# Taps of the last channels through a 128-row operand, dummy matmuls, and the order of two loads in the opening of a convolution and FFN kernel

## The chip, the cores and the metric

The kernel runs on one core of one Trainium2 chip. The metric is the device time of one execution in microseconds (us). The engines are named as in the profile: PE is TensorE's matmuls and PEld its weight loads, DVE is VectorE, ACT is ScalarE, POOL is GpSimd, SP is SyncE; a q behind the name (SPq, ACTq) is the instruction queue of that engine, where its DMAs are issued.

## The reference

Two layers run one after the other, each twice. With S = 2048 positions, D = 576 channels and F = 4608:

```python
x = A_q
x = x + A(layernorm(x), A_k, A_v, shift_k, ssm_k, ssm_D)
x = x + B(layernorm(x), w_gate, w_up, w_down)
x = x + A(layernorm(x), A_k, A_v, shift_k, ssm_k, ssm_D)
x = x + B(layernorm(x), w_gate, w_up, w_down)

# A: a causal convolution of four taps on k, times v; a long causal convolution; a gate
k_shift[s] = sum over t < 4 of k[s - t] * shift_k[:, t]      # per channel
kv = k_shift * v
y  = causal convolution of kv with ssm_k (length S), by FFT  +  kv * ssm_D
A  = q * y
# B: (gelu(x @ w_gate) * (x @ w_up)) @ w_down
```

All inputs are bf16.

## The kernel before, in words

The 2048 positions are worked on in four blocks of 512, and each block's rows as 128 partitions by four rows (`RT = 4`). The long convolution is done block by block by discrete Fourier transforms written as matmuls with tables of sines and cosines (`W` and `Wx`). The FFN's weights are streamed, and its matmuls take up nearly all of TensorE's time. A hand-written planner with cost estimates (the `Pace` object) interleaves the later blocks' convolution with the FFN of earlier blocks. The opening is different: `Conv.begin` (L856) writes its order out by hand, and the scheduling is manual, so each engine runs its instructions in the order of the text. `begin` uses no planned times, so the planner's decisions after it do not depend on what is in it.

What `begin` does, up to the point where the dense work starts:

- **Loads.** ScalarE's queue asks for `sk9` (L887, the taps as nine rows of 64 channels, given twice) and then for `dv9` (L889, D in the same form). SyncE's queue asks for the first block of k (L179, called at L888), for h, the first 512 positions of `ssm_k`, with channels on the partitions: `hn` in 4 x 128 rows (L894) and then the last 64 rows (L895); for v (L188), the tables W (L897), x (L1237), Wx (L899), the rest of W (L900), then four DMA transposes `hx` (L902) and the first FFN weights (L1224 to L1226). The semaphores by which the loads report are taken in turn.
- **Dummies.** `busy` (L912) makes matmuls of ones by ones, 256 columns each, into a tile that nobody reads (L914): ten at the start, two later.
- **Taps.** Four matmuls of the nine-row `sk9` (L920) give the taps of the first 384 channels as columns, from which VectorE makes diagonal matrices `dg` (L926). For the last 192 channels three matmuls (L931) spread a row of taps to all 128 partitions: the stationary operand is one column of the identity, broadcast, and the moving operand is the nine rows of `sk9`. ScalarE copies that to `sx` (L935).
- **k.** When k has landed, two matmuls with a shifted identity (L941) give the neighbours' rows, which ScalarE copies to `kx` (L951); twelve transposes (L949) turn the first 384 channels, which ScalarE copies to `kT` (L954), in two goes.
- **h.** `turn_h` (L978) transposes `hn` in ten pieces (L985), eight of 128 rows and two of the last 64, for two of the four row classes i at a time, and ScalarE copies the result to `hT0` (L988). In the first call `turn_d` (L959) comes between: a small transpose of `dv9` (L962) into a tile that already holds transposed k, ScalarE's copies to `dcol` (L964), and GpSimd's addition of D to the column of `hn` for time 0 (L966). The second call's half with i = 0 reads that column.
- **Convolution of four taps.** For the first 384 channels `shift_taps` (L839) multiplies by the diagonal matrices on TensorE, seven matmuls for each of three groups of 128 channels (L843); the second call of `turn_h` stands between the first and the second group. VectorE does the last 192 channels itself from `kx` and `sx` (L970 to L976), and then multiplies TensorE's results by v (L1010).
- Then come the transforms of h and of kv (L235, L242), their products, the inverse transforms (L429), the gate, the norm and the first FFN matmuls (L1708).

The matmul that the change rewrites in the taps:

```python
nc.tensor.matmul(ps[:, c // 2, c % 2 * HP * KS:(c % 2 + 1) * HP * KS],
                 lhsT=self.ident[0:NH, 2 * nt + c:2 * nt + c + 1].to_broadcast([NH, P]),
                 rhs=sk9[:, 0, :], start=True, stop=True)
```

Here `P` is 128, `NH` = 9, `HP` = 64, `KS` = 4, `nt` = 3 and c runs over the three rows of 64 channels that make up the last 192.

Of the kernel before, what the change touches and what calls it, by code (L numbers as in the profile page):

```python
# [18 lines left out]
BF16 = mybir.dt.bfloat16  # L19
# [3 lines left out]
P = 128  # L23
BS = 512
# [68 lines left out]
class Conv:  # L93
# [762 lines left out]
    def begin(self, head, tables):  # L856

        tc, nc, D, KS = self.tc, self.nc, self.D, self.KS
        nd = D // P
        width = lambda db: min(P, D - db * P)  # L860
        with ExitStack() as es:
            tmp = es.enter_context(tc.tile_pool(name="s_tmp", bufs=1))
            HP = P // 2
            NH = D // HP
            sk9 = tmp.tile([NH, 2, HP * KS], BF16, name="sk9")
            dv9 = tmp.tile([NH, 2, HP], BF16, name="dv9")
            sk9t = tmp.tile([NH, KS, HP], BF16, name="sk9t")
            hx = tmp.tile([P, RT, D], BF16, name="hx")
            dcol = tmp.tile([P, nd + 1], F32, name="dcol")
            nt = nd - 1  # L870
            DW = D - nt * P
# [5 lines left out]
            hn = tmp.tile([P, nd + 1, BS], BF16, name="hn")  # L877
# [6 lines left out]
            ones = lambda n: nc.const_aps.tensor(1.0, [P, n], BF16)  # L884

            twice = lambda src: src.unsqueeze(1).to_broadcast([NH, 2, src.shape[1]])
            nc.scalar.dma_start(out=sk9[:], in_=twice(self.sk.rearrange("(b p) j -> b (p j)", p=HP)))  # L887
            self.load_k(0, nc.sync)  # L888
            nc.scalar.dma_start(out=dv9[:], in_=twice(self.sD.rearrange("(b p) -> b p", p=HP)))  # L889
            nc.vector.memset(kT[:, :, :, 0:2], 0.0)  # L890
            nc.vector.memset(below[:, 0:1], 0.0)
            nc.vector.tensor_copy(out=below[:, 1:P], in_=self.ident[:, 0:P - 1])
            nc.scalar.activation(out=warm[:], in_=ones(1), func=ACT.Sqrt)
            nc.sync.dma_start(out=hn[:, 0:nd, :], in_=self.hk[0:nd * P, 0:BS].rearrange("(b p) t -> p b t", p=P))  # L894
            nc.sync.dma_start(out=hn[0:D - nd * P, nd, :], in_=self.hk[nd * P:D, 0:BS])  # L895
            self.load_v(0, nc.sync)
            nc.sync.dma_start(out=self.W[:, 0:12, :], in_=tables[:, 0:12, :])  # L897
            head.more(0)
# [13 lines left out]
            def busy(ps, n):  # L912
                for _ in range(n):
                    nc.tensor.matmul(ps[:, 0, 0:256], lhsT=ones(P), rhs=ones(256), start=True, stop=True)  # L914
            idle = small()
# [13 lines left out]
            ps = new()  # L929
            for c in range(DW // HP):  # L930
                nc.tensor.matmul(ps[:, c // 2, c % 2 * HP * KS:(c % 2 + 1) * HP * KS],  # L931
                                 lhsT=self.ident[0:NH, 2 * nt + c:2 * nt + c + 1].to_broadcast([NH, P]),
                                 rhs=sk9[:, 0, :], start=True, stop=True)
            for e, (lo, hi) in enumerate(((0, P), (P, DW))):
                nc.scalar.copy(out=sx[:, :, lo:hi], in_=ps[:, e, 0:(hi - lo) * KS].rearrange("p (d j) -> p j d", j=KS))  # L935
            busy(idle, 2)
            k, v = self.kt_[0], self.vt_[0]
            rest = slice(nt * P, D)
            px = new()
# [4 lines left out]
            for n, dbs in enumerate(DBS):  # L944
                pt = new_t() if n else small_t()
# [6 lines left out]
            for dbs, pt in zip(DBS, pts):  # L952
                ne = len(dbs)
                nc.scalar.copy(out=kT[:, dbs[0]:dbs[-1] + 1, :, 2:P + 2],  # L954
                               in_=pt[:, 0:ne, 0:RT * P].rearrange("p e (u q) -> p e u q", u=RT))
# [22 lines left out]
            def turn_h(pt, g, first=None):  # L978

                hv = hn[:].rearrange("p b (q i) -> p b i q", i=RT)  # L980
                for dbs in (range(nd), (nd,)):
                    for i in (2 * g + 1, 2 * g):
                        for db in dbs:
                            w = width(db)
                            nc.tensor.transpose(pt[:, i % 2, db * P:db * P + w], hv[0:w, db, i, :], self.ident[0:w, 0:w])  # L985
                if first:
                    first()
                nc.scalar.copy(out=hT0[:, 2 * g:2 * g + 2, :], in_=pt[:, :, 0:D])  # L988

            turn_h(new_t(), 1, lambda: turn_d(pts[1]))  # L990
            out = []
            for n, dbs in enumerate(DBS):
                o = (new() if n else small())[:].rearrange("p e (i c) -> p e i c", i=RT)
                for e, db in enumerate(dbs):
                    self.shift_taps(k, kT, dg, P, db, o[:, e])
                    if db == 0:
                        turn_h(new_t(), 0)
                out.append(o)
# [38 lines left out]
            def take(dst, ps, s, copy=None):  # L1037
                (copy or nc.scalar.copy)(out=self.halves(dst[:, s, :]), in_=ps[:, :, 0:HW])  # L1038

            def first(which, src, kt, s, ps):  # L1040
                if s == 0 and which is kc:
                    for k in (kt, kt + 2):
                        kc[k] = self.kcp.tile([P, 2, D], BF16, tag="kc", name="kc")
                T[src is v, kt, s] = ps
                for e in range(2):
                    self.fwd_sum(ps, src, kt, s, e)
                take(which[kt], ps, s)
# [904 lines left out]
```

## Time and profile before

| what | value |
|---|---|
| median of 3 runs | 905.81 us (905.8 to 905.88) |
| the profiled execution's own time | 905.94 us |
| its span, first to last instruction | 904.1 us |
| TensorE matmuls busy | 899.0 us, 99% of the span, 8127 instructions |
| VectorE / ScalarE / GpSimd busy | 556.9 / 329.6 / 157.9 us |
| first dense matmuls of the transform of kv | 12.64 us after the start of the span |
| first FFN matmul | 32.58 us |

The profile is one execution taken by the hardware profiler. Its views: the page (shares and groups), the chain of work that ended last, the timeline of each engine, the waits (who waited for whom), the DMA issues with the time to landing, and windows (busy time of each engine in a stretch). Times in the views are microseconds from the first instruction. In a timeline row stand the start, the length of the merged group, the engine, the line, the operation, the tiles (out<-in), the shapes and the count, and in brackets the idle time before it with what ended it. The ends of matmuls are modelled; a group's length includes the last one's tail, so the distance from one group's start to the next says more about its speed.

### The profile page before, as it was taken

How to read it: one execution, taken by the hardware profiler on the slowest of the kernel's cores; microseconds unless marked ns; L12 is line 12 of the kernel's file. 1: busy time of each engine (PE TensorE's matmuls, PEld its weight loads, DVE VectorE, ACT ScalarE, POOL GpSimd, SP SyncE). 2: the span in 40 equal slices, each digit the busy share in tenths (PEclk: the TensorE clock that was granted, in tenths of full speed). 3: DMA queues.
4: the chain of work that ended last, by engine and by line, in shares of the span. 5: the costliest groups of instructions: out<-in, count | busy, mean ns of one | idle time of the engine just before them, and what ended most of it. 6: DMA issues, size and time to landing. Idle time of an engine off the chain costs nothing.

```text
span 904.1 us, 19109 instructions
## 1 busy us (share of the span) xinstructions
PE 899.0 (99%) x8127; PEld 524.5 (58%) x8127; DVE 556.9 (62%) x957; ACT 329.6 (36%) x616; POOL 157.9 (17%) x336
## 2 busy tenths in 40 slices
PE   9999999999999999999999999999999999999998
PEld 7875646556466465564654655644444477754466
DVE  8989977678988884887898855443333322123311
ACT  7775455423322255443115133553323313022310
POOL 4423315020223031510104002310000012000000
PEclk9999999999999999999999999999999999999999
DMA  9999998567639219766915501965454431249700
GB/s 274 293 308 327 185 253 143 166 197 168 190 90 263 85 27 181 217 128 137 269 54 135 129 3 40 192 134 106 132 105 132 100 72 27 58 124 227 185 7 20
DMA packets 132075, 133.03 MB, mean 147 GB/s; under 512 B 46139, under 2 KB 123670, under 8 KB 131990
## 3 DMA queue, kind: packets, MB, share of 16 engines
q1 hardware_dynamic: 121728, 94.79, 46.7%
q0 software_dynamic: 10208, 37.02, 12.8%
q8 instruction: 63, 1.03, 0.5%
q14 instruction: 22, 0.18, 0.1%
q10 hardware_dynamic: 54, 0.01, 0.0%
HBM read 108.49 MB, written 12.39 MB: 134 GB/s over the span
## 4 chain that ended last, share of the span: by engine, by line
PE 97%; ACT 1%; DMA 0%; DVE 0%; issue 0%; DVEq 0%
PE gu L1872 60%; PE dn L1747 31%; PE gu L1708 3%; PE cps L296 1%; PE ps L235 1%; PE ps L296 0%; PE ps L429 0%; PE cps L429 0%; DMA k<-in_A_k_dram 0%; PE cps L843 0%; PE cps L235 0%; DVE v L1010 0%; PE xps L1507 0%; ACT junk L1268 0%; ACT kc L1038 0%; ACT x_c L1567 0%
## 5 line engine op out<-in xcount | busy, mean ns | idle before, releaser
L1872 PE MATMUL gu<-xnT,wgu 64*128 64x512 bf16 x4968 | 539.4, 376 | 0.0
L1872 PEld LDWEIGHTS <-wgu 64*128 64x128 bf16 x4968 | 240.2, 94 | 294.4 <-issue 4.3
L1881 ACT ACTIVATE ga<-gu 128x512 f32<-128x512 f32 x258 | 154.0, 597 | 403.9 <-PE gu L1872 395.6
L1882 DVE TENSOR_TENSOR hT<-ga,gu 128x512 bf16<-128x512 f32 x258 | 177.1, 686 | 198.8 <-ACT ga L1881 197.5
L1747 PE MATMUL dn<-wd,hT 128*128 128x288 bf16 x2304 | 290.9, 286 | 0.0
L1747 PEld LDWEIGHTS <-hT 128*128 128x128 bf16 x2304 | 224.0, 98 | 63.0 <-issue 6.4
L1260 POOL TENSOR_SCALAR nm<-s 128x1 f32<-128x1 f32 x56 | 20.4, 364 | 261.6 <-DVE x_c L1778 201.7
L1268 ACT ACTIVATE junk<-x_c,nm 128x576 bf16<-128x576 f32 x48 | 37.0, 770 | 44.9 <-POOL nm L1260 43.9
L1769 DVE TENSOR_TENSOR ob<-x_c,dn 128x576 bf16<-128x576 f32 x15 | 11.3, 754 | 67.6 <-PE dn L1747 67.6
L574 POOL DMA_DIRECT2D hr<-Hd x32 | 17.5, 547 | 117.7 <-DVE prod L375 117.0
L1276 POOL TENSOR_TENSOR rstd<-ve,neghalf_t 128x1 f32<-128x1 f32 x58 | 36.9, 637 | 4.8
L1786 DVE TENSOR_TENSOR x_c<-x_c,dn 128x576 f32<-128x576 f32 x38 | 28.6, 752 | 5.5 <-PE dn L1747 5.2
L1332 ACT ACTIVATE xn<-x_c,nb,rstd 128x576 bf16<-128x576 f32 (+1 forms) x48 | 28.6, 645 | 9.1 <-POOL nb L1280 8.9
L1275 POOL TENSOR_SCALAR ve<-ss 128x1 f32<-128x1 f32 x58 | 20.4, 352 | 47.0 <-ACT junk L1268 46.9
L299 ACT COPY eo<-cps 128x576 f32<-128x576 f32 x29 | 18.7, 643 | 27.3 <-PE cps L296 24.0
L1778 DVE SCALAR_TENSOR_TENSOR x_c<-dn,x_c 128x576 f32<-128x576 f32 x16 | 12.1, 754 | 26.0 <-PE dn L1747 26.0
L1687 ACT ACTIVATE ga<-gu 128x512 bf16<-128x512 f32 x26 | 15.5, 598 | 30.5 <-PE gu L1872 25.9
L1708 PE MATMUL gu<-xnT,wgu 64*128 64x256 bf16 x432 | 24.8, 269 | 0.3 <-ACT xnT L1514 0.3
L444 POOL DMA_DIRECT2D out_dram<-ob x12 | 6.8, 564 | 97.7 <-DVE ob L1769 97.7
L1708 PEld LDWEIGHTS <-wgu 64*128 64x128 bf16 x432 | 21.4, 94 | 3.2 <-issue 1.2
L376 DVE TENSOR_TENSOR prod<-prod 128x576 bf16<-128x576 bf16 x48 | 22.0, 458 | 1.6
L259 DVE SCALAR_TENSOR_TENSOR eo<-eo 128x576 f32<-128x576 f32 x22 | 16.3, 753 | 5.8 <-ACT eo L299 5.8
(182 smaller groups left out, 587.2 us busy)
## 6 DMA issues: line engine op xcount, KB each, us to landing
wgu<-in_B_w_gate_dram SPq DMA_DIRECT2D x45, 576.0 KB, 5.7
wd<-in_B_w_down_dram SPq DMA_DIRECT2D x30, 864.0 KB, 9.1
wgu<-in_B_w_up_dram SPq DMA_DIRECT2D x45, 512.0 KB, 8.2
hr<-Hd POOLq DMA_DIRECT2D x32, 288.0 KB, 5.8
kr<-Kd POOLq DMA_DIRECT2D x24, 288.0 KB, 5.7
Kd<-kc POOLq DMA_DIRECT2D x12, 288.0 KB, 6.6
k<-in_A_k_dram POOLq DMA_DIRECT2D x3, 1008.0 KB, 9.9
wgu<-in_B_w_up_dram SPq DMA_DIRECT2D x45, 64.0 KB, 7.7
```

Of the source, the lines that this page charges most:

```text
L376: nc.vector.tensor_tensor(out=dst, in0=pr[:, 0, :], in1=pr[:, 1, :], op=ALU.subtract if part == 0 else ALU.add)
L1260: nc.gpsimd.tensor_scalar(out=v["nm"][:], in0=v["s"][:], scalar1=-1.0 / D, scalar2=None, op0=ALU.mult)
L1268: nc.scalar.activation(out=junk[:], in_=get_x(), func=ACT.Square, bias=v["nm"][:, 0:1], accum_out=v["ss"][:])
L1275: nc.gpsimd.tensor_scalar(out=ve[:], in0=v["ss"][:], scalar1=1.0 / D, scalar2=EPS, op0=ALU.mult, op1=ALU.add)
L1276: nc.gpsimd.tensor_tensor(out=v["rstd"][:], in0=ve[:], in1=neghalf_t[:, 0:1], op=ALU.pow)
L1332: nc.scalar.activation(out=xn[:, lo:hi], in_=x_c[c][:, j, 0:hi - lo], func=ACT.Identity, scale=v["rstd"][:, 0:1], bias=v["nb"][:, 0:1])
L1708: nc.tensor.matmul(pair[:, s, e * 256:(e + 1) * 256], lhsT=w[r0:r0 + HK, k, gi * P:(gi + 1) * P], rhs=xnT[r0:r0 + HK, blk_of[k], tok], sta ...
L1747: nc.tensor.matmul(part[h][:, h, 0:HW], lhsT=hT[:, f, at * P:(at + 1) * P], rhs=wd[2 * wk + f // WT][:, f % WT, h * HW:(h + 1) * HW], star ...
L1786: nc.vector.tensor_tensor(out=xh, in0=xh, in1=acc[:, :, 0:HW], op=ALU.add)
L1872: nc.tensor.matmul(pair[:, s, :], lhsT=w[r0:r0 + HK, k, gi * P:(gi + 1) * P], rhs=xnT[r0:r0 + HK, b, :], start=(k == 0), stop=(k == NKC - 1))
L1881: nc.scalar.activation(out=ga[:], in_=pair[:, 0, :], func=ACT.Gelu_apprx_tanh)
L1882: nc.vector.tensor_tensor(out=hT[:, fi, :], in0=ga[:], in1=pair[:, 1, :], op=ALU.mult)
```

## The change

Four edits, all in `begin`:

1. A new tile `skb` of 128 rows is set to zero on VectorE, and rows 6 to 8 of the taps (three rows of 256 elements, the last 192 channels) are loaded into its first three rows, by ScalarE's queue, between `sk9` and `dv9`. The three matmuls that spread the taps use `skb` and a full column of the identity in place of the nine-row `sk9`.
2. The two dummies in front of the work on k become three.
3. The load of the last 64 rows of h is issued before that of the 512 others.
4. In the first call of `turn_h`, behind `turn_d`, three dummy transposes of the identity are written to a part of the tile that nobody reads.

```diff
+            skb = tmp.tile([P, HP * KS], BF16, name="skb")
...
-            nc.scalar.dma_start(out=sk9[:], in_=twice(self.sk.rearrange("(b p) j -> b (p j)", p=HP)))
+            rows = self.sk.rearrange("(b p) j -> b (p j)", p=HP)
+            nc.vector.memset(skb[:], 0.0)
+            nc.scalar.dma_start(out=sk9[:], in_=twice(rows))
+            nc.scalar.dma_start(out=skb[0:DW // HP, :], in_=rows[2 * nt:NH, :])
             self.load_k(0, nc.sync)
...
+            nc.sync.dma_start(out=hn[0:D - nd * P, nd, :], in_=self.hk[nd * P:D, 0:BS])
             nc.sync.dma_start(out=hn[:, 0:nd, :], in_=self.hk[0:nd * P, 0:BS].rearrange("(b p) t -> p b t", p=P))
-            nc.sync.dma_start(out=hn[0:D - nd * P, nd, :], in_=self.hk[nd * P:D, 0:BS])
             self.load_v(0, nc.sync)
...
             for c in range(DW // HP):
                 nc.tensor.matmul(ps[:, c // 2, c % 2 * HP * KS:(c % 2 + 1) * HP * KS],
-                                 lhsT=self.ident[0:NH, 2 * nt + c:2 * nt + c + 1].to_broadcast([NH, P]),
-                                 rhs=sk9[:, 0, :], start=True, stop=True)
+                                 lhsT=self.ident[:, c:c + 1].to_broadcast([P, P]), rhs=skb[:], start=True, stop=True)
...
-            busy(idle, 2)
+            busy(idle, 3)
...
                 if first:
                     first()
+                    for _ in range(3):
+                        nc.tensor.transpose(pt[:, 1, 7 * P:8 * P], self.ident[:], self.ident[:])
                 nc.scalar.copy(out=hT0[:, 2 * g:2 * g + 2, :], in_=pt[:, :, 0:D])
```

## The prediction

> **What bounds the kernel now.** I read the page first, then the chain of work that ended last in order of time, then the opening by engine in the timeline. From the page's part 4:
>
> ```profile
> PE 97%; ACT 1%; DMA 0%; DVE 0%; issue 0%; DVEq 0%
> ```
>
> TensorE is the chain for 97% of the span: whatever the first microseconds do, the rest follows as one block. The question is when that block may start, and the chain of the opening (start, length, what) says it:
>
> ```profile
> 0.73 3.81 DMA k<-in_A_k_dram
> ...
> 7.67 0.17 PE pt L962
> 7.83 1.28 PE cps L843 x7
> 9.11 0.64 PE pt L985 x10
> 9.75 0.99 PE cps L843 x7
> ...
> 12.64 1.14 PE cps L235 x8
> ```
>
> The first block of k lands at 4.54; its transposes and ScalarE's copies of them, the transposes of D (L962), the taps as matmuls (L843) and VectorE's product with v (L1010) follow, and at 12.64 the dense part begins. From there to the first FFN matmuls at 32.58 the chain names TensorE, ScalarE and VectorE and no transfer. A gain at 12.64 should reach the end, and so should a loss.
>
> TensorE's rows in the timeline (start, length of the group, engine):
>
> ```profile
> 0.77 2.29 PE L914 MATMUL cps<-const-bfloat16-1.0 128*128 128x256 bf16 x10 [0.77 <-PEq L1936]
> 3.03 0.29 PE L920 MATMUL ps<-ident,sk 9*128 9x6 bf16 x4
> 3.18 0.80 PE L931 MATMUL ps<-sk,ident 9*128 9x256 bf16 x3
> 3.91 0.61 PE L914 MATMUL cps<-const-bfloat16-1.0 128*128 128x256 bf16 x2
> 4.59 0.64 PE L941 MATMUL ps<-k,below 128*128 128x384 bf16 x2
> 5.02 1.06 PE L949 MATMUL cpt<-ident,k 128*128 128x128 bf16 x8
> 5.88 0.63 PE L949 MATMUL pt<-ident,k 128*128 128x128 bf16 x4
> 6.30 1.28 PE L985 MATMUL pt<-ident,hn 128*128 128x128 bf16 x10
> ...
> 7.76 1.35 PE L843 MATMUL cps<-dg,kT 128*128 128x512 bf16 x7
> 8.95 0.81 PE L985 MATMUL pt<-ident,hn 128*128 128x128 bf16 x10
> 9.69 1.05 PE L843 MATMUL cps<-dg,kT 128*128 128x512 bf16 x7
> 10.57 1.03 PE L843 MATMUL ps<-dg,kT 128*128 128x512 bf16 x7
> ```
>
> Two speeds are in these rows. A group's length has the last matmul's tail in it, so I go by starts. Eight transposes of k take 5.88 - 5.02 = 0.86 us, 107 ns each; all ten of h later take 9.69 - 8.95 = 0.74 us, pauses included. Seven tap matmuls take 8.95 - 7.76 = 1.19 us the first time and 10.57 - 9.69 = 0.88 us afterwards. TensorE ran at half rate until about 8.4, inside the first taps; at full rate a transpose is 107 / 2, some 55 ns. (The page's clock row reads 9 in the first slice too; here the matmuls' own spacing decides.)
>
> **What raised the clock.** In the 3.8 us before the rise, from 4.59 to 8.41, full-row work filled: the pair of L941 0.43 us, 20 transposes at 0.107 = 2.14, the first part of L843 0.65: 3.2 us. In the 3.8 us before that, from 0.77 to 4.59, it was 12 dummies at 0.21 = 2.5 us, beside L931's three matmuls of nine rows (0.6 us) and some pauses, and the clock did not rise. So 3.2 in 3.8 us was enough and 2.5 was not, and nine rows did not make up the difference.
>
> **The change part by part.**
>
> *Taps on 128 rows, one more dummy.* L931's three matmuls keep their 256 columns (0.21 us each) but use 128 rows; the third dummy adds 0.21 us. The stretch to 4.59 then holds 13 + 3 matmuls at 0.21 = 3.4 us of full-row work, more than the 3.2 that sufficed. Does the dummy delay k? Two end at 3.91 + 2 x 0.21 = 4.33, three at 4.54, and L941 waits for k until 4.59: it costs nothing, with 0.05 us to spare. When does the clock rise? Bounds from the rows: not before 3.2 us of such work are done, about 4.35, and at the latest at 8.41 as now. I take 5.0, nearer the early end because the work exceeds what sufficed, and not at it because the rows show one rise and not how soon it follows the work. [...]
>
> *What full rate from 5.0 is worth.* ScalarE's rows:
>
> ```profile
> 5.26 0.70 ACT L951 CAST kx<-ps 128x384 bf16<-128x384 f32 x2 [0.39 <-PE ps L941]
> 6.12 1.01 ACT L954 COPY kT<-cpt 128x1024 bf16<-128x1024 bf16 x1 [0.15 <-PE cpt L949]
> 7.03 0.59 ACT L954 COPY kT<-pt 128x512 bf16<-128x512 bf16 x1
> ...
> 8.10 0.32 ACT L964 CAST dcol<-pt 64x5 f32<-64x5 bf16 x2
> ```
>
> The eight transposes end 8 x 0.05 = 0.4 us sooner, near 5.65 instead of 6.08. But ScalarE is busy with kx until 5.96, so the first copy of kT moves only by about its idle 0.15 us, from 6.12 to 5.95. The second copy moves with it, and so does L962, whose tile that copy reads: from 7.67 to about 7.5. Behind L962 stand the three new dummies, 3 x 0.055 = 0.17 us, so L843 starts at 7.73 instead of 7.76; at full rate it needs 0.88 and ends at 8.6 instead of 8.95. The next transposes of h (L985) then have to wait, for their half with i = 0 reads what GpSimd has added D to:
>
> ```profile
> 8.50 0.73 POOL L966 TENSOR_TENSOR hn<-hn,dcol 128x4 bf16<-128x4 bf16 x2 [7.20 <-ACT dcol L964]
> ```
>
> That follows ScalarE's dcol and so moves by ScalarE's 0.18 us alone: the long first addition ends near 8.9, the second at 9.05 instead of 9.23. TensorE, through with the half i = 1 at 8.8, waits there. So L985, the second L843 and VectorE's L1010 all move by 0.18 us; TensorE's gain of 0.35 us is cut to what ScalarE gives. VectorE lets this much through:
>
> ```profile
> 10.77 1.23 DVE L1010 TENSOR_TENSOR v<-cps,v 128x1024 bf16<-128x1024 f32 x1 [0.54 <-PE cps L843]
> ```
>
> It is idle for 0.54 us before L1010. That is also the most that the change can bring, since nothing shortens VectorE's chain before it.
>
> *The three dummies behind D.* They stand in TensorE's queue ahead of both L843 and the L985 between. At full rate they cost 0.17 us, of which the wait for GpSimd just named covers nearly all; at half rate 0.32 us, with nothing to cover it.
>
> *The new load of skb.* ScalarE's queue issues it behind sk9, in the place that dv9 has now; dv9 follows some 0.3 us later.
>
> ```profile
> 0.72 0.59 ACTq L887 DMA_DIRECT2D sk<-in_A_shift_k_dram  x1
> 1.35 0.28 ACTq L889 DMA_DIRECT2D dv<-in_A_ssm_D_dram  x1
> ```
>
> ```profile
> SPq L902 <- DMA dv<-in_A_ssm_D_dram: 0.4, 1, 0.4
> ```
>
> ```profile
> 5.33 7.44 SPq L902 DMA_TRANSPOSE hx<-in_A_ssm_k_dram  x4
> ```
>
> This is the change's new wait. Behind L931 are queued the dummies and all of TensorE's work on k; ScalarE waits for L931 with sx, and VectorE behind sx. Bounds: sk9 had landed when L920 started, 3.03 - 0.72 = 2.3 us after its issue; by that skb lands at 3.65. dv9 landed at 5.33, when hx stopped waiting for it, 4.0 us after its issue and behind the 512 KB of hn; by that skb lands at 5.3. Ahead of skb there stand only sk9, k and perhaps the 64 rows of h, not hn. It is three rows of 512 bytes, a sixth of sk9, so it need not wait for sk9's slowest part: I take 3.1, in time for L931, and keep both ends. Its memset on VectorE comes third in that queue, ahead of small ones, and has until the issue at 1.35.
>
> The wait row shows one more thing: hx, the eleventh load, waits for dv9, the third, that is for the landing of the one eight places older. With skb in between, Wx waits for skb instead of sk9. Should that hold Wx and hx up even to 5.3, the weights behind hx still have until 32.58; it costs nothing.
>
> *The last 64 rows of h first.*
>
> ```profile
> hn<-in_A_ssm_k_dram SPq DMA_DIRECT2D x1, 512.0 KB, 4.7
> ...
> hn<-in_A_ssm_k_dram SPq DMA_DIRECT2D x1, 64.0 KB, 5.6
> ```
>
> The small part now lands 5.6 us after its issue, at 1.66 + 5.6 = 7.25, and the first L985's last two transposes wait for it; asked for first, it lands near 5. The 512 KB come later than 1.19 + 4.7 = 5.9 by an eighth at most, 0.6 us. TensorE is through with k at 5.7 and waits until 6.1 to 6.5; eight transposes and the two small ones then end by 7.1, still ahead of L962 at 7.5, which ScalarE sets. Nothing won, nothing lost. v's issue on SP's queue keeps its place behind the same two.
>
> *Sum.* 0.18 us. The profiled execution took 905.94 with a span of 904.1 (1.8 around it); it becomes 905.76. The median of the runs is 0.13 lower than the profiled one: 905.81 becomes **905.6**. With the clock already up at 4.4 the pair of L941 is faster too, and the gain comes near VectorE's 0.54: 905.3.
>
> **The rivals.**
>
> *skb comes late* (ends slower). It decides at 3.2 us: beyond that, each 0.1 us holds L931, the three dummies and all work on k back by 0.1. At 3.65 L941 starts 0.45 later and the clock's 0.18 does not pay for it: 906.1. At 5.3, like dv9, it starts 2.1 later: 907.9. For it: dv9's 4.0 us from that very place in the queue. Against it: hn is no longer ahead.
>
> *The clock stays as it is.* The transposes are then as slow as now, and of the dummies' 0.32 us some 0.1 comes back since more of L843 falls behind 8.4: +0.2, 906.0. For it: one rise is all the trace has, and 3.4 and 3.2 are close.
>
> *The clock rises and falls again.* With transposes twice as fast TensorE is busy for less of the time from 5.0 to 8.4: by the lengths of the rows above, halved, some 2.7 of 3.4 us. A fall there puts a stretch such as 8.4 to 12.2 at half rate, and about half its 3.4 us of matmuls, 1.7 us, is lost: 907.3. Against it, a later stretch (length, then TensorE's busy time) and what follows it:
>
> ```profile
> 29.00:32.50 3.50, 2.78 (x30) 1.92 (x29) 3.36 (x11) 2.94 (x7) 0.00 (x0) 1.00 1.07 284
> ```
>
> ```profile
> 32.58 8.04 PE gu L1708 x144
> ```
>
> That stretch is as thin, and yet the 144 matmuls of 256 columns behind it took 56 ns each, two at a time on 64 rows: full rate. [...]
>
> **How the numbers follow.** Forecast 0.60; skb late 0.20, half of it beyond 906.7; clock unchanged 0.13; clock falls 0.05; something else 0.02. The range goes from the early clock less 0.2 us, 905.1, to 906.7, which takes in the unchanged clock and the milder late landings. A measurement of this kernel can tell about 0.2%, 1.8 us, from no change. Faster by that is shut out by VectorE's 0.54 us, and I leave 0.01; slower by that needs dv9's landing time or a falling clock, 0.06; the other 0.93 lies within.
>
> **What would show it.** Right: L949's transposes 55 ns apart, the first kT copy at 5.95, the first L843 in 0.88 us, L1010 at 10.6, the first FFN matmul at 32.4. skb late: L931 starts after 3.2 and L941 after 4.6. Clock unchanged: L949 at 107 ns, L843 near 8.1. Clock falls: L843's second group takes over 1.5 us. Wrong altogether would be a stage after 12.64 that moves by another amount than L1010 does.

## The result, and the profile after

The changed kernel takes 908.48 us (median of 7 runs, 907.68 to 909.81) against 905.87 for the kernel before (7 runs, 905.51 to 906.76): a ratio of 1.0029, interval 1.0019 to 1.0039, so slower by 2.6 us. The forecast was 905.6. The profiled execution took 909.35 with a span of 907.6, 3.4 us above the profiled one of before, so it shows somewhat more than the median does.

The line of the page by engine, and the chain of work that ended last (start, length, what); line numbers are shifted by up to five:

```profile
PE 97%; ACT 1%; DMA 1%; DVE 0%; SPq 0%; issue 0%
```

```profile
1.18 0.57 SPq L898
1.75 0.05 issue
1.80 6.34 DMA hn<-in_A_ssm_k_dram
8.15 0.05 issue
8.19 1.27 PE pt L988 x10
9.46 0.12 PE pt L965
9.58 0.43 PE pt L992 x3
10.01 1.71 PE cps L843 x7
11.71 1.08 PE pt L988 x10
12.79 1.01 PE cps L843 x7
...
15.70 1.14 PE cps L235 x8
...
36.04 8.04 PE gu L1713 x144
```

Before, the chain began with k; now it begins with the 512 rows of h, which land at 8.15 instead of 5.9, although they are asked for only 0.6 us later. TensorE's rows in the timeline:

```profile
3.49 0.29 PE L924 MATMUL ps<-ident,sk 9*128 9x6 bf16 x4 [0.43 <-DMA sk<-in_A_shift_k_dram]
3.97 0.82 PE L935 MATMUL ps<-skb,ident 128*128 128x256 bf16 x3 [0.19 <-DMA skb<-in_A_shift_k_dram]
4.58 0.85 PE L918 MATMUL cps<-const-bfloat16-1.0 128*128 128x256 bf16 x3
5.22 0.69 PE L944 MATMUL ps<-k,below 128*128 128x384 bf16 x2
5.70 1.06 PE L952 MATMUL cpt<-ident,k 128*128 128x128 bf16 x8
6.55 0.63 PE L952 MATMUL pt<-ident,k 128*128 128x128 bf16 x4
8.19 1.27 PE L988 MATMUL pt<-ident,hn 128*128 128x128 bf16 x10 [1.00 <-DMA hn<-in_A_ssm_k_dram]
9.39 0.18 PE L965 MATMUL pt<-ident,dv 9*128 9x9 bf16 x1
9.51 0.50 PE L992 MATMUL pt<-ident 128*128 128x128 bf16 x3
9.80 1.92 PE L843 MATMUL cps<-dg,kT 128*128 128x512 bf16 x7
11.51 1.28 PE L988 MATMUL pt<-ident,hn 128*128 128x128 bf16 x10
12.72 1.06 PE L843 MATMUL cps<-dg,kT 128*128 128x512 bf16 x7
```

The difference to before at each start tells where the time came in. L944: 5.22 against 4.59, +0.63: the taps wait first for sk9 (0.43 us, until 3.49) and then for skb (0.19 us, until 3.97), and six matmuls of 0.21 us stand between them and k. In this execution k itself landed only at 5.10 instead of 4.54, which alone would have put L944 near 5.15, so little of the 0.63 is due to the taps. First L988: 8.19 against 6.30, +1.89, waiting for h. First L843: 9.80 against 7.76, +2.04, with the three dummies taking 9.80 - 9.51 = 0.29 at half rate. Second L843: 12.72 against 9.69, +3.03: the first taps take 1.71 us instead of 1.19 and the ten transposes 1.21 instead of 0.74, since TensorE ran at half rate until 12.8. The transform of kv starts at 15.70, +3.06; the first FFN matmul at 36.04, +3.46. So another 0.4 us came in between those two, which has a cause of its own (below).

### The profile page after: what moved, and what is told of

It is laid out like the page before. It is cut to its first block, busy times and chain, and to the rows that moved or that the text cites. A ratio compares the mean times of both kernels' runs of the same rounds, so it can differ in the third digit from the quotient of the medians.

```text
span 907.6 us, 19119 instructions
## 1 busy us (share of the span) xinstructions
PE 900.6 (99%) x8131; PEld 525.9 (58%) x8131; DVE 557.1 (61%) x958; ACT 329.8 (36%) x616; POOL 156.9 (17%) x336
## 4 chain that ended last, share of the span: by engine, by line
PE 97%; ACT 1%; DMA 1%; DVE 0%; SPq 0%; issue 0%
PE gu L1877 59%; PE dn L1752 31%; PE gu L1713 3%; PE cps L296 1%; DMA hn<-in_A_ssm_k_dram 1%; PE ps L235 1%; PE ps L296 0%; PE ps L429 0%; PE cps L429 0%; PE cps L843 0%; PE pt L988 0%; PE cps L235 0%; DVE v L1015 0%; PE xps L1512 0%; ACT junk L1273 0%; ACT kc L1043 0%
## 5 line engine op out<-in xcount | busy, mean ns | idle before, releaser
L259 DVE SCALAR_TENSOR_TENSOR eo<-eo 128x576 f32<-128x576 f32 x22 | 16.3, 753 | 5.8 <-ACT eo L299 5.8
```

## The experiments

Medians in us of 5 to 11 runs each; "before" is the kernel before, timed beside them (905.87 beside the changed kernel, 906.05 to 906.18 beside the others). Each difference given below is to the median of before from the same group of runs. Differences under about 0.9 us lie inside their intervals one by one; there I go by the medians with the trace beside them.

| run | median | ratio, interval | taps start | L941 starts | 512 rows of h land | clock up at | kv transform starts |
|---|---|---|---|---|---|---|---|
| before | 906.06 | | 3.18 | 4.59 | 5.93 | 8.4 | 12.64 |
| changed kernel | 908.48 | 1.0029 (1.0019 to 1.0039) | 3.97 | 5.22 | 8.15 | 12.8 | 15.70 |
| h_first | 909.01 | 1.0033 (1.0020 to 1.0045) | 3.15 | 4.74 | 8.25 | 13.9 | 16.11 |
| skb_alone | 908.03 | 1.0021 (1.0012 to 1.0029) | 4.99 | 6.03 | 6.63 | 10.7 | 14.51 |
| dummies | 906.02 | 1.0000 (0.9991 to 1.0009) | 3.14 | 4.58 | 5.90 | 9.5 | 13.30 |
| after_h_back | 908.26 | 1.0024 (1.0014 to 1.0033) | 5.14 | 6.40 | 5.99 | 9.0 | 14.50 |
| copy_taps | 905.57 | 0.9996 (0.9987 to 1.0005) | 3.22 | 4.55 | 5.84 | 5.3 | 12.11 |
| copy_full | 905.70 | 0.9993 (0.9984 to 1.0002) | 3.22 | 4.56 | 6.17 | 6.9 | 12.62 |
| skb_pool | 909.47 | 1.0038 (1.0025 to 1.0050) | 6.27 | 7.31 | 6.06 | 12.2 | 15.90 |
| h64_act | 906.28 | 1.0000 (0.9991 to 1.0008) | 3.14 | 4.56 | 5.98 | 9.7 | 13.35 |
| after_copy | 909.00 | 1.0031 (1.0019 to 1.0043) | 3.22 | 4.58 | 8.64 | 4.0, down 7.4, up 14.3 | 16.67 |
| hbig_act | 912.27 | 1.0055 (1.0036 to 1.0075) | 3.15 | 4.60 | 11.90 | 16.3 | 19.17 |
| one_memset | 906.56 | 1.0007 (0.9998 to 1.0016) | 3.15 | 4.57 | 5.86 | 7.4 | 12.60 |
| copy_pool_zero | 905.87 | 0.9995 (0.9986 to 1.0004) | 3.22 | 4.53 | 5.92 | 4.0 | 12.48 |

Columns four on are from each run's one profiled execution, in us from its start; the landing is the last count on the load's semaphore, and the clock's rise is where the trace's record of full clock begins, which the spacing of the matmuls bears out.

**One part at a time.**

h_first, only the order of the two loads:

```diff
+nc.sync.dma_start(out=hn[0:D - nd * P, nd, :], in_=self.hk[nd * P:D, 0:BS])
 nc.sync.dma_start(out=hn[:, 0:nd, :], ...)
-nc.sync.dma_start(out=hn[0:D - nd * P, nd, :], in_=self.hk[nd * P:D, 0:BS])
```

> The kernel before with only the two loads of h exchanged. Theory 1 (the order of h costs most): the 512 KB land near 7 to 8 us instead of 5.9, TensorE stands still after the transposes of k until then, L985 starts 1 us or more later than 6.30, and the median is 0.8 to 1.5 us above before. Theory 2 (the late taps cost most, the order matters only behind them): the 512 KB land by 6.5, L985 loses at most 0.3 us, the time is within 0.2 us of before.

Measured: +2.95 us, twice the most that theory 1 expected, and no less than the whole change costs. Its timeline:

```profile
6.02 0.63 PE L949 MATMUL pt<-ident,k 128*128 128x128 bf16 x4
8.29 1.26 PE L985 MATMUL pt<-ident,hn 128*128 128x128 bf16 x10 [1.64 <-DMA hn<-in_A_ssm_k_dram]
```

TensorE stands still for 1.64 us, and then the first taps run at half rate (1.68 us, 9.61 to 11.29, against 1.19 before). Are the DMA engines full meanwhile? The windows from 4 to 7 us (the last two columns are the DMA engines' share and GB/s), first of h_first, then of before:

```profile
4.00:5.00 1.00, 0.74 (x3) 0.26 (x2) 1.00 (x7) 0.84 (x2) 0.00 (x0) 1.00 0.48 113
5.00:6.00 1.00, 1.00 (x10) 0.98 (x9) 1.00 (x5) 0.59 (x2) 0.00 (x0) 1.00 0.76 230
```

```profile
4.00:5.00 1.00, 0.93 (x4) 0.43 (x5) 1.00 (x7) 0.86 (x2) 0.00 (x0) 1.00 1.07 364
5.00:6.00 1.00, 1.00 (x12) 0.99 (x11) 1.00 (x5) 0.70 (x2) 0.00 (x0) 1.00 1.10 232
```

They are half idle while the 512 rows are outstanding: 0.48 and 113 GB/s from 4 to 5 us, in which the last of k lands (4.70), and 0.76 in the next microsecond. In this stretch the load is not late for want of bandwidth; its rows do not get to the engines. The trace's DMA packets say the same: by 5.0 us 400 of the 576 rows of h had started to move in before, 135 in h_first. Later they do meet company: from 7 to 8 us, with v under way as well, the share is 1.00.

skb_alone, only the 128-row taps:

```diff
+nc.vector.memset(skb[:], 0.0)
 nc.scalar.dma_start(out=sk9[:], in_=twice(rows))
+nc.scalar.dma_start(out=skb[0:DW // HP, :], in_=rows[2 * nt:NH, :])
...
-   lhsT=self.ident[0:NH, 2 * nt + c:2 * nt + c + 1].to_broadcast([NH, P]), rhs=sk9[:, 0, :]
+   lhsT=self.ident[:, c:c + 1].to_broadcast([P, P]), rhs=skb[:]
```

> The kernel before with only the taps through 128 rows (new load, zeroing, the three matmuls), two dummies as before, no dummies behind D, h in the old order. Theory 1: skb lands by 3.3 or its lateness hides in the wait for k; within 0.3 us of before. Theory 2: the three tap matmuls start near 4.0 instead of 3.18, the dummies end after k has landed, L941 starts near 5.0 instead of 4.59, and the median is 0.4 to 1 us above before.

Measured: +1.97 us, theory 2 and beyond it.

```profile
4.99 0.82 PE L935 MATMUL ps<-skb,ident 128*128 128x256 bf16 x3 [1.71 <-DMA skb<-in_A_shift_k_dram]
5.60 0.63 PE L918 MATMUL cps<-const-bfloat16-1.0 128*128 128x256 bf16 x2
6.03 0.68 PE L944 MATMUL ps<-k,below 128*128 128x384 bf16 x2
```

With h in its old order skb lands at 4.94, 3.6 us after its issue (dv9 took 4.0 from that place); in the changed kernel, where the 512 rows come behind it, at 3.92. Some 0.4 of the 1.97 us is the pause of VectorE that has its own part below.

dummies:

```diff
-busy(idle, 2)
+busy(idle, 3)
...
 first()
+for _ in range(3):
+    nc.tensor.transpose(pt[:, 1, 7 * P:8 * P], self.ident[:], self.ident[:])
```

> The kernel before with only the dummies: three instead of two in front of k and three transposes behind D's turn. Theory 1 and 2 alike: L941 still starts by 4.65; behind D the three cost 0.17 us at full rate and 0.32 at half rate, of which part is hidden; 0 to 0.3 us above before. Theory 3 (the dummies themselves are what the change pays for): 0.8 us or more above before.

Measured: -0.04 us, no change; theory 3 falls. Its profiled execution, with 906.62 one of the slowest of its 11 runs, shows the 0.29 us behind D at half rate.

after_h_back undoes the order of h alone in the changed kernel:

```diff
-nc.sync.dma_start(out=hn[0:D - nd * P, nd, :], in_=self.hk[nd * P:D, 0:BS])
 nc.sync.dma_start(out=hn[:, 0:nd, :], ...)
+nc.sync.dma_start(out=hn[0:D - nd * P, nd, :], in_=self.hk[nd * P:D, 0:BS])
```

> The changed kernel with the loads of h back in the old order, all else changed. Theory 1: the 512 KB land near 6 again, L985 starts right behind k's transposes, and 1 us or more of the 2.6 comes back: 1.0 to 1.6 us above before. Theory 2: no more than 0.3 us comes back: 2.3 us or more above before.

Measured: 2.2 us above before, so 0.4 of the 2.6 us came back (0.2 if the two medians are compared directly). That lies between the two theories, close to theory 2. But theory 1 was right about the cause and wrong to add: the order costs 2.95 alone, the taps 1.97 alone, both together 2.6. Late taps push k's transposes back into the time in which TensorE would wait for h anyway: the wait is 1.64 us in h_first and 1.00 in the changed kernel.

**The taps without a load.** In copy_taps VectorE copies what sk9 brought into the zeroed tile:

```diff
+nc.vector.memset(skb[:], 0.0)
...
+nc.vector.tensor_copy(out=skb[0:NH, :], in_=sk9[:, 0, :])
...
+   lhsT=self.ident[:, 2 * nt + c:2 * nt + c + 1].to_broadcast([P, P]), rhs=skb[:]
...
+busy(idle, 3)
```

> The taps through 128 rows without a load of their own: VectorE copies the nine rows of sk9 into a zeroed tile, and the matmuls pick rows 6 to 8; three dummies in front of k, none behind D, h in the old order. If the late load is what the 128-row taps cost (theory A): the taps start at 3.2 to 3.3, L941 by 4.65, and the cost of 2 us against before is gone. If then full-row work raises the clock (theory B, the prediction's step): L949 runs at full rate or the rise comes before 7, and the median is 0.1 to 0.5 us below before. If the clock stays (theory C): within 0.1 us of before, the rise no earlier than 8.

Measured: 905.57, 0.48 us below before: theories A and B.

```profile
3.22 0.82 PE L934 MATMUL ps<-skb,ident 128*128 128x256 bf16 x3
3.83 0.85 PE L916 MATMUL cps<-const-bfloat16-1.0 128*128 128x256 bf16 x3
4.55 0.64 PE L943 MATMUL ps<-k,below 128*128 128x384 bf16 x2
4.99 0.75 PE L951 MATMUL cpt<-ident,k 128*128 128x128 bf16 x8
5.58 0.39 PE L951 MATMUL pt<-ident,k 128*128 128x128 bf16 x4
...
6.84 0.26 PE L987 MATMUL pt<-ident,hn 64*128 64x64 bf16 x2 [0.32 <-DMA hn<-in_A_ssm_k_dram]
...
7.48 1.05 PE L843 MATMUL cps<-dg,kT 128*128 128x512 bf16 x7
```

The clock rises at 5.3, among k's transposes: eight of them in 0.59 us. VectorE's product with v then starts without an idle time before it, at 10.23 instead of 10.77:

```profile
9.64 0.56 DVE L978 TENSOR_TENSOR v<-wx,v 128x768 bf16<-128x768 bf16 x1
10.23 1.23 DVE L1012 TENSOR_TENSOR v<-cps,v 128x1024 bf16<-128x1024 f32 x1
```

That is the full 0.54 us that the prediction named as the most the change could bring, in an execution that was one of this kernel's fastest (905.40; its 11 runs go from 905.39 to 906.00). This is the version with the lowest median of all. That it beats the kernel before is likely by medians and trace and not beyond the noise, since its interval reaches from 0.9987 to 1.0005.

copy_full is copy_taps with the three dummies behind D's turn as well, so the whole change without its new load and without the exchange of the loads of h:

```diff
 first()
+for _ in range(3):
+    nc.tensor.transpose(pt[:, 1, 7 * P:8 * P], self.ident[:], self.ident[:])
```

> The same with the three dummies behind D's turn as well, so the changed kernel without its new load and without the exchange of the loads of h. Theory A: within 0.5 us of before, all of the 2.6 us were the two loads. If instead the dummies or the 128-row matmuls carry a part of it: 0.8 us or more above before. Against the run without the dummies behind D: 0.0 to 0.3 us slower.

Measured: 905.70. Theory A: all of the 2.6 us is the doing of the new load and the exchange, and by the medians the rest would have brought 0.35. The dummies behind D add 0.13 by the medians; the ratios to before (0.9993 here, 0.9996 for copy_taps) stand the other way round, so this is not resolved. In the profiled execution nothing is gained at the transform of kv (12.62 against 12.64), for the clock rose only at 6.9, behind k's transposes, and the first copy of kT moved by 0.03 us. Then comes a new wait:

```profile
7.48 0.25 PE L987 MATMUL pt<-ident,hn 64*128 64x64 bf16 x2 [0.31 <-DMA hn<-in_A_ssm_k_dram]
```

With faster transposes TensorE runs into the load of the last 64 rows of h. They landed at 6.80 in copy_taps, at 7.44 here and at 7.58 in copy_pool_zero, where TensorE waited 1.0 us for them, and the first taps on TensorE (L843) started at 7.48, at 7.95 (behind the three dummies as well) and at 7.92. So part of the gain hangs on that landing.

**Why the loads are late.** skb_pool is skb_alone with skb issued from GpSimd's queue:

```diff
-nc.scalar.dma_start(out=skb[0:DW // HP, :], in_=rows[2 * nt:NH, :])
+nc.gpsimd.dma_start(out=skb[0:DW // HP, :], in_=rows[2 * nt:NH, :])
```

> The 128-row taps with their load issued by GpSimd's queue instead of ScalarE's; two dummies, h in the old order. [...] Theory A2 (any second small load is late beside k and h, the engines being full): it lands at 4.5 or later, and the time is 1.5 us or more above before.

Measured: +3.4 us; skb lands at 6.23, 4.8 us after its issue. Theory A2 by its number; why it is later still than from ScalarE's queue (4.94 in skb_alone), no run shows. h64_act is the kernel before with the small load of h moved to ScalarE's queue, behind sk9:

```diff
+nc.scalar.dma_start(out=hn[0:D - nd * P, nd, :], in_=self.hk[nd * P:D, 0:BS])
 nc.scalar.dma_start(out=dv9[:], ...)
...
-nc.sync.dma_start(out=hn[0:D - nd * P, nd, :], in_=self.hk[nd * P:D, 0:BS])
```

> The kernel before with the load of the last 64 rows of h taken from SyncE's queue to ScalarE's, between sk9 and dv9; SyncE asks for the 512 rows right behind k, as before. Theory O1 (the 512 rows were late because they were issued 0.6 us later and behind another load on SyncE's queue): they land by 6.3, L985 starts by 6.6, within 0.3 us of before or faster. Theory O2 (any load of rows ahead of them or beside them delays them): they land at 7.5 or later, and the time is 1.5 us or more above before.

Measured: +0.2 us, the 512 rows at 5.98, theory O1: asked for at 1.18 they are on time. hbig_act turns that round: the 512 rows on ScalarE's queue, asked for at 1.35, the 64 on SyncE's at 1.19:

```diff
+nc.scalar.dma_start(out=hn[:, 0:nd, :], in_=self.hk[0:nd * P, 0:BS].rearrange("(b p) t -> p b t", p=P))
 nc.scalar.dma_start(out=dv9[:], ...)
...
-nc.sync.dma_start(out=hn[:, 0:nd, :], in_=self.hk[0:nd * P, 0:BS].rearrange("(b p) t -> p b t", p=P))
```

> The kernel before with the 512 rows of h asked for by ScalarE's queue behind sk9, at about 1.36, and the 64 rows by SyncE's queue behind k, at 1.19. Theory P (the 512 rows are late when they are issued late, or behind another load on the same queue): they land by 6.5 and the time is within 0.4 us of before. Theory G (both queues' loads are generated in one order, and a load of rows ahead of the 512 delays them whatever queue it is on): they land at 7.5 or later, and the time is 1.5 us or more above before.

Measured: 912.27; the 512 rows land at 11.90. Theory G in its outcome. They were asked for only 0.17 us later than before, and 0.45 us earlier than in the changed kernel, and came later than in either. One of the six runs took 906.54, the others 911.8 to 913.0; no trace shows that run.

```profile
5.89 0.63 PE L949 MATMUL pt<-ident,k 128*128 128x128 bf16 x4
11.95 1.26 PE L985 MATMUL pt<-ident,hn 128*128 128x128 bf16 x10 [5.43 <-DMA hn<-in_A_ssm_k_dram]
```

Here the DMA engines were not idle: their share was 0.95 to 1.07 in each microsecond from 5 to 9 us, and 349 of the 576 rows had started by 5.5 us, the last only at 11.4, while other loads were moving. So the place behind k (5.98 with it in h64_act, 11.90 without it here) matters far more than the bytes ahead. What inside the DMA path holds a load with 512 rows back once another stands between it and k stays open.

after_copy keeps the changed kernel's order of h and takes only the new load out (copied taps, all dummies); beside copy_full:

```diff
-nc.sync.dma_start(out=hn[:, 0:nd, :], ...)
 nc.sync.dma_start(out=hn[0:D - nd * P, nd, :], ...)
+nc.sync.dma_start(out=hn[:, 0:nd, :], ...)
```

> The changed kernel with its load of skb replaced by VectorE's copy from sk9; the loads of h stay exchanged and all dummies stay. If the exchange alone costs 2.9 us and the late taps are hidden behind it (the two delays lie beside each other): the 512 KB land near 8, and the time is 2 to 3 us above before. If the late taps also set the time of the changed kernel: 1 us or more below the changed kernel, 1.5 us or less above before.

Measured: 909.00, 2.8 above before: the first alternative. It also shows the clock falling. The windows (first the stretch and its length, then TensorE's busy time; last but two the granted clock):

```profile
4.10:7.40 3.30, 1.40 (x17) 0.97 (x15) 3.23 (x14) 3.21 (x8) 0.00 (x0) 1.00 0.80 261
7.50:14.20 6.70, 5.52 (x35) 3.71 (x36) 2.55 (x5) 2.53 (x5) 0.43 (x2) 0.50 1.08 308
14.30:20.00 5.70, 5.64 (x48) 4.26 (x47) 4.79 (x12) 3.13 (x7) 1.83 (x4) 1.00 1.02 218
```

The clock was up at 4.0; TensorE then had 1.40 us of work in 3.3 and waited for h until 8.68; at 7.4 the clock went down and came back at 14.3, after taps and transposes.

**The other 0.4 us.** VectorE's rows at the gate's first step (the second row of each pair), of after and then of before:

```profile
29.07 0.45 DVE L396 TENSOR_TENSOR yb<-yb 128x576 bf16<-128x576 bf16 x1
30.37 0.82 DVE L1579 SCALAR_TENSOR_TENSOR x_c<-ps,scale_t,x_c 128x576 f32<-128x576 f32 x1 [0.86 <-ACT scale_t L1552]
```

```profile
26.01 0.45 DVE L396 TENSOR_TENSOR yb<-yb 128x576 bf16<-128x576 bf16 x1
26.91 0.82 DVE L1574 SCALAR_TENSOR_TENSOR x_c<-ps,scale_t,x_c 128x576 f32<-128x576 f32 x1 [0.46 <-ACT junk L1546]
```

VectorE is idle for 0.86 instead of 0.46 us before the gate. The wait in VectorE's queue ahead of it ends 0.40 us behind the row above in both, and the releaser that the row of after names (scale_t) ended later than that wait did, so it is not the cause. All four kernels with the new load have this pause. one_memset is the kernel before with nothing but the zeroing of an unused tile on VectorE:

```diff
+skb = tmp.tile([P, HP * KS], BF16, name="skb")
...
+nc.vector.memset(skb[:], 0.0)
```

> The kernel before with one instruction more on VectorE, the zeroing of a tile that nothing uses. All four kernels with the load of skb, which have one VectorE instruction more than before, need 20.34 us from the first matmul of the transform of kv to the first FFN matmul; the others need 19.94, and the 0.4 us lie in a pause of VectorE before its gate that no wait explains. If the pause hangs on the place of that instruction in VectorE's stream: 20.34 here too, 0.3 to 0.5 us above before. If it hangs on the load or on the late taps: 19.94, within 0.15 us of before.

Measured: 906.56, +0.44, and 20.35 us between the two matmuls, though the transform of kv starts on time at 12.60: the place in the stream. The gate's row shows the pause:

```profile
27.29 0.82 DVE L1576 SCALAR_TENSOR_TENSOR x_c<-ps,scale_t,x_c 128x576 f32<-128x576 f32 x1 [0.87 <-ACT scale_t L1549]
```

copy_pool_zero moves copy_taps' zeroing to GpSimd:

```diff
-nc.vector.memset(skb[:], 0.0)
+nc.gpsimd.memset(skb[:], 0.0)
```

> The copied taps with the zeroing on GpSimd instead of VectorE, so one VectorE instruction more than before instead of two. If the pause hangs on the place in VectorE's stream: 20.34 us between the same two matmuls, and 0.3 to 0.5 us slower than with the zeroing on VectorE. If it does not: 19.94, and 0.1 us of it at most.

Measured: 19.94 us and 905.87, 0.25 below before where copy_taps is 0.48 below: the pause is not there, and the theory as it was put failed. (The smaller gain is in line with the late 64 rows of h named above.) I had counted computing instructions only. Counted with the waits that VectorE's queue holds, the gate is VectorE's 64th instruction in the five kernels with the pause (changed kernel, skb_alone, after_h_back, skb_pool, one_memset), where it starts 0.46 us after the wait before it, and the 63rd, 65th or 66th in the nine others, copy_pool_zero among them, where it starts 0.06 us after. In those nine the 64th is the instruction behind the gate's, the wait itself or the product ahead of it, and none of these starts late. The place goes with the pause in all fourteen, and one_memset, which changes nothing else, brings it about. Why the 64th, the traces do not say; the count with the waits was found after the runs, and no run was made to test it.

## Why the prediction was wrong

The step that failed first is "The last 64 rows of h first ... Nothing won, nothing lost". It bounded the delay of the 512 rows by bytes, 0.6 us at most. Measured were 2.2 us (8.15 against 5.93), with the DMA engines at 0.47 and 0.74 of their time from 4 to 6 us in the changed kernel; h_first shows it alone to cost 2.95 us. What the bytes ahead would take is thus not what sets the landing; why the load loses so much by its place stays open.

The second is skb, "I take 3.1, in time for L931". It landed at 3.92 in the changed kernel and at 4.94 with h in its old order. The rival "skb comes late" was right in mechanism and in the deciding point. Its price can't be read off the changed kernel, where k landed late as well and L988 stood waiting for h until 8.19 whatever came before it: after_copy, without the load of skb, is no faster (2.8 us above before, against 2.6). Alone, in skb_alone, the late load costs 1.97 us, 0.4 of it by VectorE's pause, against the 2.1 that the rival gave for a landing at 5.3. Its chance of 0.20 was too small: the row of dv9 came from that very place in the queue, and the argument that hn was no longer ahead held only together with the other edit that did the harm.

The step on the clock was right where its condition held, "3.2 in 3.8 us was enough" and 128-row taps that arrive in time. My 5.0 was an estimate between two bounds, and no run shows it: the four kernels with copied taps have full clock at 4.0, 4.0, 5.3 and 6.9, the four with nine-row taps and no long wait at 7.4, 8.4, 9.5 and 9.7 (one_memset, before, dummies, h64_act). That nine rows did not make up the difference can be worked out more closely from the rows, each matmul counted at the half rate (0.107 us for 128 columns), in stretches of 3.41 us (a length that after_copy shows, below) that end with the rise. The stretch that ends with the first rise held at least 2.7 us of full-row work in every kernel, and none of the stretches of this length ahead of it held more than 2.5. In dummies the last stretch but one, 2.63 to 6.04, held 2.3 us of full-row and 0.6 us of nine-row work, and the clock stayed down; in copy_pool_zero 2.9 us, all of it on full rows, brought it up. In the changed kernel the pauses for sk9, for skb and for h kept that much work from coming together until 12.8, which costs about 1 us in the taps and the transposes behind them.

The 0.18 us, what full rate is worth, was mis-sized, and the runs scatter around it. By the medians copy_taps, which has no dummies behind D, gains 0.48 of the 0.54 us named as the limit, and copy_full, which has them, 0.35; in copy_full's profiled execution there is no gain. In copy_taps the first copy of kT moved from 6.12 to 5.82, by 0.30 and not by ScalarE's idle 0.15, and GpSimd's two additions took 0.41 us instead of 0.73, so that the second transposes of h did not wait for them.

When the clock rises differs from execution to execution: the four kernels with copied taps do the same work on TensorE up to 4.5 us, and their rises lie up to 2.8 us apart. In after_copy rise, fall and rise lie 3.41 and 6.83 us apart. The second is twice the first; what sets these distances, the traces do not say. Most of the work ahead of a rise can be transposes: in after_h_back the clock rose at 9.0, and the last 2.1 of the 3.41 us before that were nothing but transposes, with 1.3 us of other matmuls ahead of them. In after_copy, after 1.40 us of work in 3.3, the clock fell.

The rival in which the clock falls again came about in after_copy, by the wait for h (3.02 us) and not by faster transposes; in copy_taps and copy_full the clock held (granted 1.00 in the windows 7.45 to 14.2 and 14.3 to 20 us). The dummies behind D cost 0.29 us at half rate (0.32 worked out) and 0.17 at full rate, as worked out; over the medians 0.0 (beside before) and 0.13 (copy_taps to copy_full).

Nothing in the prediction foresaw that one more instruction on VectorE would cost 0.4 us at 30 us. It held that a gain or loss at 12.64 would reach the end unchanged; it did so in the nine kernels without that pause, with 19.94 to 19.95 us to the first FFN matmul. In the changed kernel it did not, and this is the sign that the prediction itself had named, "a stage after 12.64 that moves by another amount than L1010 does": VectorE's product with v moved by 3.06 us (10.77 to 13.83), the first FFN matmul by 3.46.

## What to carry to other kernels

When the order of loads at the start of a kernel is changed, don't reckon the delay in bytes: take the landing time of whatever stood in that place in the queue before (the 64 rows that were second behind k landed at 7.25, and the 512 rows in their place at 8.15), and be ready for a load of many rows to lose microseconds (2.2 in the changed kernel, 6.0 in hbig_act) when it is no longer the one right behind the first. A tiny load can be an expensive way to get data that another load has already brought: skb took 2.6 to 4.8 us to land, VectorE's copy 0.2. And two delays before the same wait did not add up here (2.95 and 1.97 us alone, 2.6 together), so undoing one of them showed little: 0.4 us in after_h_back, nothing in after_copy.

## What the runs showed of the hardware that was not expected

- A load of 512 rows of 1 KB, asked for at 1.2 us right behind k, lands at 5.8 to 6.6; asked for at 1.8 behind one of 64 rows, at 8.2 to 8.6, with the DMA engines at 0.47 and 0.48 of their time from 4 to 5 us (changed kernel, h_first); asked for at 1.35 on the other queue, with the 64 rows at 1.19 on the first, at 11.9.
- In the five kernels where the gate is VectorE's 64th instruction, waits counted, it starts 0.4 us later behind its wait than in the nine others. In those the 64th is not an instruction behind a wait, and it starts without such a pause.
- The same stream of matmuls (up to 4.5 us) got its full clock at 4.0 in one execution and at 6.9 in another.
- Matmuls of nine rows did not help to raise the clock: 2.3 us of full-row and 0.6 us of nine-row work in 3.4 us left it down, 2.7 us of full-row work raised it (as worked out above, one trace each).
